# A two-layer transformer stack on one core: smaller work buffers, eight weight slots for eleven, 74 resident weight pieces for 68, a new order, and the local output projection in five chunks

## The chip, the cores and the metric

The kernel runs on one NeuronCore of a Trainium2 chip. The metric is the device time of one launch in microseconds; the time of a kernel is the median over several launches. Five engines work side by side and meet through semaphores: TensorE (PE, with its weight loads listed as PEld), VectorE (DVE), ScalarE (ACT), GpSimd (POOL) and SyncE (SP). SP here does nothing but issue weight transfers. Sixteen DMA engines carry all transfers between HBM and the on-chip memory SBUF; matrix products land in PSUM, which has eight banks.

## The reference

Two layers alternate, each used twice, on 2048 tokens of width 640, with a layer norm and a residual sum around each:

```python
x = x + _A_ref(_layernorm(x), A_mem0, A_Wq, A_Wk, A_Wv, A_Wo, A_seg_len)
x = x + _B_ref(_layernorm(x), B_wqkv, B_wo)
x = x + _A_ref(...)      # the same weights again
x = x + _B_ref(...)
```

Layer A is recurrent. The tokens come in 64 segments of 32. Eight memory rows are put in front of a segment, full attention with 32 heads of 192 runs over the 40 rows (causal behind the memory), and the eight first output rows are the memory of the next segment:

```python
for s in range(n_seg):
    h = concatenate([mem, xs[s]]);  q, k, v = h @ Wq, h @ Wk, h @ Wv
    p = softmax(where(mask, q @ k.T * scale, -1e9));  o = (p @ v) @ Wo
    mem = o[:, :M];  outs.append(o[:, M:])
```

Layer B is local attention: 32 heads of 20, each token sees eight tokens at distances 0, 2, ..., 14, then an output projection of 640 by 640.

## The kernel before

Both passes of A run at once, as two lanes of one matrix product: lane 0 has segment t of the first pass, lane 1 segment t - 2 of the second (LAG = 2). So a lane has 40 columns and a projection of A moves NT = 80 columns through each 128 by 128 weight block. In the first two steps and the last two of A only one lane is live. A step is one segment; there are 66 with A, and one more that has only B. B for the segment pair of step t - 1 runs inside step t.

A's heads are worked in eight quads of four heads. A step has these pieces, named in the string ORDER with the quad's number: K, Q, V (30 weight blocks each: project), KE, QE, VE (copy from PSUM to SBUF: KE and VE on ScalarE, QE on VectorE), T and TE (transpose V, copy), S (scores), E (exp, ScalarE), EM (mask, VectorE), PD (denominators), R (their reciprocals, as exp of minus Ln, both on ScalarE), PO (probabilities times V), OT1 and OT2 (divide, VectorE), Oa and Ob (output projection, 15 blocks each, into the two banks acc0 and acc1). Quad 7's output projection is split into O7x, O7y and O7z, so that acc0 is complete before acc1. MEMa and MEMb write the new memory rows from acc0 and acc1 into the next step's input hT; K0 of the next step reads it. X1 makes A's residual sum, BSQ its squares. LSQ, lst, LMV, LR and LAP are the layer norm of the next segment. Names in small letters are B's: bst to bap its layer norm, bq, bk, bv projections with bqE, bkE, bvE, then bt and btE, qx (queries spread over heads), bs (scores), be (exp, ScalarE), eb (mask, VectorE), bp and on (times V, divide), bo and boE (transpose), by (output projection) and byE (residual sum).

ORDER is a list written out in full. Each engine gets its instructions in that order and works them one after another; a piece waits only for semaphores of what it reads, and for the last readers of the buffers it writes. Five PSUM banks ("big") go round in the order in which pieces ask for them.

A's weights are 64 halves of 15 blocks, each half cut into pieces of 8 and 7 blocks (256 KB and 224 KB): 128 pieces. N_RES = 68 of them stay in SBUF after their first load in step 0. The other 60 are loaded again in each step, into a ring of RING = 11 slots (load_piece, the DMA is on line 220): SP issues the next transfer when TensorE is done with the slot's last content, and when the transfer eight before it has landed, because eight semaphores go round. `resident_pieces` picks the resident ones evenly by their number in the order of use. B's weights wqkv and wo are loaded once, after step 0.

Lines that matter below: 242 the projections of A, 361 its output projection, 391 the memory rows, 451 bq and bk, 552 bo, 566 by, 511 be and 522 eb, 332 R, 349 to 355 OT1 and OT2.

Of the kernel before, what the change touches and what calls it, by code (L numbers as in the profile page):

```python
# [17 lines left out]
P = 128  # L18
D = 640
# [26 lines left out]
PD0 PO0 R0 OT10 bq E1 Q4 bqE S2 EM1 V3 bv qx1 T2 QE4 E2 OT20 bk VE3 PO1 bvE qx0 PD1 T3 bkE K3 TE2 EM2 TE3 R1  # L46
KE3 bs0 be0 K4 OT11 OT21 bs1 be1 KE4 V5 Q3 QE3 eb1 PO2 VE5 bs3 PD2 V4 R2 qx2 S4 OT12 be3 VE4 E4 eb0 bs2 Oa1 S3
bt E3 EM4 K5 Q5 btE be2 bs5 eb3 Oa0 EM3 QE5 PD3 bs4 KE5 Q6 eb2 be5 eb5 OT22 Ob0 T4 S5 QE6 R3 PD4 be4 E5 PO3
eb4 OT13 K6 Ob1 TE4 bp1 T5 R4 V6 bp0 OT23 on1 PO4 KE6 TE5 EM5 VE6 S6 OT14 K7 Q7 E6 PD5 on0 OT24 T6 KE7 bo Oa2
# [16 lines left out]
def half_blocks(kind, i, h):  # L66
# [9 lines left out]
    return blocks[15 * h:15 * (h + 1)]  # L76

def resident_pieces():
    pieces = [u + (q,) for u in half_order() for q in range(2)]
    return {u for n, u in enumerate(pieces) if (n * N_RES) // len(pieces) != ((n + 1) * N_RES) // len(pieces)}  # L80

class Kernel:
# [25 lines left out]
    def build_consts(self):  # L108
# [24 lines left out]
        self.VT = pers("VT", [P, 6 * NT + 48], 2)  # L133
        self.x1 = pers("x1", [P, NC, NX], 2)
        self.h2T = pers("h2T", [P, NC, P], 1)[0]
        self.KB = pers("KB", [P, NBC, P], 1)[0]
# [6 lines left out]
        self.wqkv = cp.tile([P, NC, 3 * D], BF16, name="wqkv_sb")  # L143
        self.wo = cp.tile([P, 2, 3, D], BF16, name="wo_sb")

# [47 lines left out]
    def load_b_weights(self):  # L193
        nc = self.nc
        nc.sync.dma_start(out=self.wqkv[:].rearrange("p c n -> p (c n)"), in_=self.b_src[0])
        nc.sync.dma_start(out=self.wo[:].rearrange("p a m n -> p (a m n)"), in_=self.b_src[1])

# [112 lines left out]
    def sE(self, i):  # L310
        cs = self.cs
        e = self.ap1.tile([P, 4, NT], BF16, name="E", tag=f"E{i % 2}")
        self.nc.scalar.activation(out=e[0:NT, :, cs], in_=self.sv[i][0:NT, :, cs], func=ACT.Exp, scale=float(DH) ** -0.5)  # L313
        self.e[i] = e

    def sM(self, i):
        cs, w = self.cs, self.cs.stop - self.cs.start
        em = self.ap1.tile([P, 4, NT], BF16, name="Em", tag=f"Em{i % 2}")
        self.nc.vector.tensor_tensor(out=em[0:NT, :, cs], in0=self.e[i][0:NT, :, cs],  # L319
                                     in1=self.maskA[0:NT, cs].unsqueeze(1).to_broadcast([NT, 4, w]), op=ALU.mult)  # L320
        self.em[i] = em

# [109 lines left out]
    def b_x1(self, b):  # L432
        nc = self.nc
        x1 = self.x1[b % 2]
        ls = slice(self.l0, self.l1)
        for g, c in enumerate((slice(0, 3), slice(3, NC))):
            nc.vector.tensor_tensor(out=x1[:, c].rearrange("p c (l n) -> p c l n", l=2)[:, :, ls, :], in0=self.acc_lanes(g)[:, :, ls, NM:LT],
                                    in1=self.xin[b % 2][:, c].rearrange("p c (l n) -> p c l n", l=2)[:, :, ls, :], op=ALU.add)
        self.acc = None

    def b_ln_apply(self, b):
        self.ln_big(self.x1[b % 2], self.bmr, self.h2T[:, :, 64 * (b % 2):64 * (b % 2) + NX].rearrange("p c (l n) -> p c l n", l=2))

    def b_proj(self, b, col0, name):
        nc = self.nc
        ps = self.big(name)
        h = self.h2T[:, :, 64 * (b % 2):64 * (b % 2) + NX]
        for n in range(NBC):
            for c in range(NC):
                e0 = col0 + BHC * BD * n  # L450
                nc.tensor.matmul(ps[:, NX * n:NX * (n + 1)], lhsT=self.wqkv[:, c, e0:e0 + P], rhs=h[:, c, :],  # L451
                                 start=(c == 0), stop=(c == NC - 1))
        return ps
# [8 lines left out]

    def b_v(self, b):
        nc = self.nc
        ps = self.big("ps_bv")
        hs = slice(64 * (b % 2), 64 * (b % 2) + NX)
        for n in range(NC):
            for c in range(NC):
                e0 = 2 * D + P * n
                nc.tensor.matmul(ps[:, NX * n:NX * (n + 1)], lhsT=self.wqkv[:, c, e0:e0 + P], rhs=self.h2T[:, c, hs],  # L470
                                 start=(c == 0), stop=(c == NC - 1))
# [29 lines left out]
    def b_s(self, c):  # L501
# [4 lines left out]
        self.bsp[c] = ps  # L506

    def b_e(self, c):
        nh = min(BHC, BH - BHC * c)
        e = self.ap1.tile([P, BHC, NX], BF16, name="eraw", tag=f"eraw{c % 2}")  # L510
        self.nc.scalar.activation(out=e[:, 0:nh, :].rearrange("p h n -> p (h n)"), in_=self.bsp[c][:, 0:nh * NX], func=ACT.Exp, scale=float(BD) ** -0.5)  # L511
        self.be[c] = e

    def b_m(self, b, c):
        nc, e = self.nc, self.be[c]
        nh = min(BHC, BH - BHC * c)
        mask = self.maskB_first.get(b, self.maskB[b % 2])
        h = BHC * c
        end = h + nh
        while h < end:  # L520
            n = min(end, 16 if h < 16 else 32) - h
            nc.vector.tensor_tensor(out=self.eb[:, h % 16:h % 16 + n, h // 16, :], in0=e[:, h - BHC * c:h - BHC * c + n, :],  # L522
                                    in1=mask[:].unsqueeze(1).to_broadcast([P, n, NX]), op=ALU.mult)
            h += n

# [10 lines left out]
    def b_on(self, g):  # L536
        nc = self.nc
        pv = self.bpv[g]
        on = self.On[:, 0:D // 2].rearrange("p (h d) -> p h d", d=BD)
        r = self.ap2.tile([P, 8, 1], F32, name="rB")  # L540
        nc.vector.reciprocal(out=r[:], in_=pv[:, :, BD:BD + 1])
        for par in range(2):
            rows = slice(64 * par, 64 * par + 64)
            d0 = (BD + 1) * par
            nc.vector.tensor_tensor(out=on[rows, 8 * g:8 * g + 8, :], in0=pv[rows, :, d0:d0 + BD],  # L545
                                    in1=r[rows].to_broadcast([64, 8, BD]), op=ALU.mult)

    def b_ot(self):
        nc = self.nc
        ps = self.big("ps_bt")  # L550
        for m in range(3):
            nc.tensor.matmul(ps[:, P * m:P * (m + 1)], lhsT=self.On[:, P * m:P * (m + 1)], rhs=self.ident[:], start=True, stop=True)  # L552
        self.bop = ps

    def b_oE(self):
        ob = self.bp.tile([P, 3, P], BF16, name="OTB")
        self.nc.scalar.copy(out=ob[:], in_=self.bop[:, 0:3 * P].rearrange("p (m n) -> p m n", m=3))  # L557
        self.otb = ob

    def b_wo(self):  # L560
        nc = self.nc
        ps = self.big("ps_by")
        for n in range(NC):
            for k in range(6):
                par, m = k % 2, k // 2
                nc.tensor.matmul(ps[:, NX * n:NX * (n + 1)], lhsT=self.wo[:, par, m, P * n:P * (n + 1)],  # L566
                                 rhs=self.otb[:, m, 64 * par:64 * par + 64], start=(k == 0), stop=(k == 5))
        self.byp = ps

    def b_yE(self, b):  # L570
        nc = self.nc
        x1 = self.x1[b % 2]
        pv = self.byp[:, 0:NC * NX].rearrange("p (c n) -> p c n", c=NC)
# [21 lines left out]
    def prologue(self):  # L595
        nc = self.nc
        self.xt, self.ots, self.qxs, self.kp, self.qp, self.vp, self.tp = {}, {}, {}, {}, {}, {}, {}
        self.qt, self.e, self.em, self.r, self.bsp, self.be, self.bpv, self.sv, self.dn = {}, {}, {}, {}, {}, {}, {}, {}, {}
        self.acc = None
# [20 lines left out]
    def b_piece(self, n, b):  # L620
        k, g = n[:2], n[2:]
        if n == "bst":
            self.bsp_ = self.ln_stats(self.x1[b % 2], self.bsq)
        elif n == "bmv":
# [13 lines left out]
        elif n == "bv":  # L638
            self.b_v(b)
        elif n == "bvE":  # L640
# [27 lines left out]
    def a_piece(self, n, t):  # L668
# [8 lines left out]
        if n == "BSQ":  # L677
            self.bsq = self.ln_sq(self.x1[t % 2])
            return
# [63 lines left out]
def laid_out(A_x, A_mem0, A_Wq, A_Wk, A_Wv, A_Wo, B_wqkv, B_wo):  # L743
# [41 lines left out]
```

## Time and profile before

| | |
|---|---|
| median of 6 runs | 3391.9 us (3387.08 to 3402.63) |
| the profiled execution's own time | 3396.63 us |
| its span, first to last instruction | 3394.9 us |
| mean granted TensorE clock | 0.985 |
| HBM read, written | 1000.25 MB, 2.62 MB |
| step 0, step 1 | 83.7 us, 48.2 us |
| steps 5 to 63, together | 2971.0 us |

The page of the profile gives for each engine its busy time, share of the span and number of instructions, and for each DMA queue the packets, megabytes and share of the sixteen engines' span. A row of a group reads: line, engine, operation, output and inputs, shapes, count, then busy us and mean ns of one, then the idle time of the engine before it and what ended that. A row of the waits reads: who waited for whom, us in total, times, longest us. A row of the DMA issues ends in KB each and the median us from issue to landing. A row of the timeline begins with start and length in us.

### The profile page before, as it was taken

To read this page: it belongs to the slowest core of one execution; us is meant where nothing else is said; L and a number is where in the kernel's file an instruction comes from. 1 tells how busy PE (TensorE), PEld (TensorE's weight loads), DVE (VectorE), ACT (ScalarE), POOL (GpSimd) and SP (SyncE) were. 2 spreads that over 40 slices of the span, in tenths; PEclk is the share of its full clock that TensorE was granted. 3 is DMA by queue.
4 is the path that set the end of the run, shared out by engine and by line. 5 is a ranking of instruction groups with operands and counts; after the bars stand their busy time and mean duration, and the time that the engine had idled before them with its cause. 6 is when DMAs were issued, how large, how long until landed. Compare 5 with 4: busy or idle time off the path is not lost. (4 is left out here: it accounts for less than half of the span.)

```text
span 3394.9 us, 194049 instructions
## 1 busy us (share of the span) xinstructions
PE 3222.4 (95%) x86394; PEld 3145.7 (93%) x86394; DVE 2060.2 (61%) x6355; ACT 1742.1 (51%) x4621; POOL 40.7 (1%) x150
## 2 busy tenths in 40 slices
PE   5799999999999999999999999999999999999997
PEld 4799999999999999999999999999999999999986
DVE  2466665666666666566666666666656656656655
ACT  1355455455555555555545555555555555555543
POOL 2000000000000000000000000000000000000000
PEclk6899999999999999999999999999999999999998
DMA  9989999899999998898998999999899889889896
GB/s 326 334 299 300 301 295 300 302 297 310 297 303 300 305 308 292 299 306 291 301 306 293 305 300 305 301 299 306 292 296 299 295 295 305 294 294 303 285 308 217
DMA packets 585910, 1015.55 MB, mean 299 GB/s; under 512 B 65136, under 2 KB 310384, under 8 KB 584944
## 3 DMA queue, kind: packets, MB, share of 16 engines
q1 hardware_dynamic: 580320, 997.88, 88.3%
q8 instruction: 677, 11.09, 1.3%
q10 hardware_dynamic: 4752, 5.26, 0.4%
q14 instruction: 161, 1.32, 0.1%
HBM read 1000.25 MB, written 2.62 MB: 295 GB/s over the span
## 5 line engine op out<-in xcount | busy, mean ns | idle before, releaser
L242 PEld LDWEIGHTS <-w_ring 128*128 128x128 bf16 x22506 | 994.5, 100 | 61.0 <-issue 31.9
L277 DVE CAST QT<-ps_q 128x480 bf16<-128x480 f32 (+1 forms) x528 | 339.2, 642 | 470.9 <-PE ps_q L242 443.4
L349 DVE TENSOR_TENSOR OT<-ps_o,R 128x320 bf16<-128x320 f32 (+1 forms) x528 | 254.2, 481 | 303.4 <-ACT R L332 177.9
L282 ACT CAST VT_107<-ps_v 128x480 bf16<-128x480 f32 (+1 forms) x264 | 144.2, 546 | 413.6 <-PE ps_v L242 412.0
L313 ACT ACTIVATE E<-ps_s 80x320 bf16<-80x320 f32 (+1 forms) x528 | 223.2, 423 | 251.4 <-PE ps_s L307 251.2
L361 PEld LDWEIGHTS <-w_ring 128*128 128x128 bf16 x7326 | 331.1, 100 | 13.1 <-issue 4.9
L331 ACT ACTIVATE R<-ps_d 128x320 f32<-128x320 f32 (+1 forms) x528 | 226.5, 429 | 221.6 <-PE ps_d L325 218.9
L332 ACT ACTIVATE R<-R 128x320 f32<-128x320 f32 (+1 forms) x528 | 243.9, 462 | 16.7
L296 DVE COPY Vt_103<-ps_vt 80x384 bf16<-80x384 bf16 x528 | 163.3, 349 | 136.9 <-PE ps_vt L288 134.8
L242 PE MATMUL ps_q<-hT_88,w_ring 128*128 128x80 bf16 (+1 forms) x4026 | 231.3, 201 | 8.2 <-issue 6.0
L242 PE MATMUL ps_q<-hT_90,w_ring 128*128 128x80 bf16 (+1 forms) x4026 | 229.7, 201 | 5.4 <-issue 4.0
L242 PE MATMUL ps_v<-hT_88,w_ring 128*128 128x80 bf16 (+1 forms) x3795 | 218.6, 201 | 8.6 <-issue 4.2
L242 PE MATMUL ps_v<-hT_90,w_ring 128*128 128x80 bf16 (+1 forms) x3795 | 217.5, 201 | 7.0 <-issue 5.5
L282 ACT CAST VT_105<-ps_v 128x480 bf16<-128x480 f32 (+1 forms) x264 | 143.6, 544 | 155.5 <-PE ps_v L242 155.1
L242 PE MATMUL ps_k<-hT_90,w_ring 128*128 128x80 bf16 (+1 forms) x3432 | 197.6, 200 | 11.1 <-DMA w_ring<-in_wA_dram 8.6
L242 PE MATMUL ps_k<-hT_88,w_ring 128*128 128x80 bf16 (+1 forms) x3432 | 198.9, 201 | 5.3 <-DVE hT_88 L429 2.4
L271 ACT CAST KF_95<-ps_k 128x320 bf16<-128x320 f32 (+1 forms) x264 | 110.1, 417 | 179.3 <-PE ps_k L242 179.3
L271 ACT CAST KF_93<-ps_k 128x320 bf16<-128x320 f32 (+1 forms) x264 | 110.2, 418 | 165.9 <-PE ps_k L242 165.9
L319 DVE TENSOR_TENSOR Em<-E,maskA 80x320 bf16<-80x320 bf16 (+1 forms) x528 | 165.0, 313 | 43.5 <-ACT E L313 31.3
L296 DVE COPY Vt_101<-ps_vt 80x384 bf16<-80x384 bf16 x528 | 161.3, 345 | 43.4 <-PE ps_vt L288 43.4
L511 ACT ACTIVATE eraw<-ps_bs 128x384 bf16<-128x384 f32 (+1 forms) x396 | 175.3, 446 | 19.6 <-PE ps_bs L505 16.9
L355 DVE TENSOR_TENSOR OT<-ps_o,R 64x160 bf16<-64x160 f32 (+1 forms) x528 | 170.3, 322 | 7.2
(2830 smaller groups left out, 8699.9 us busy)
## 6 DMA issues: line engine op xcount, KB each, us to landing
w_ring<-in_wA_dram SPq DMA_DIRECT2D x2112, 256.0 KB, 4.7
w_ring<-in_wA_dram SPq DMA_DIRECT2D x1848, 224.0 KB, 4.8
out_dram<-YT_125 ACTq DMA_DIRECT2D x16, 160.0 KB, 5.4
wqkv_sb<-in_wqkv_dram SPq DMA_DIRECT2D x1, 2400.0 KB, 10.2
wo_sb<-in_wo_dram SPq DMA_DIRECT2D x1, 960.0 KB, 12.0
w_k_00_550<-in_wA_dram SPq DMA_DIRECT2D x1, 256.0 KB, 5.1
w_k_10_569<-in_wA_dram SPq DMA_DIRECT2D x1, 256.0 KB, 5.1
w_q_00_592<-in_wA_dram SPq DMA_DIRECT2D x1, 256.0 KB, 5.1
```

The costliest lines, as they stand in the source:

```text
L242: self.nc.tensor.matmul(ps[:, NT * n + c0:NT * n + c1], lhsT=self.block(kind, i, h, k), rhs=hT[:, NT * c + c0:NT * c + c1], start=(h == 0 ...
L271: nc.scalar.copy(out=kf[:, :, :, cs], in_=pv[:, :, 0:3:2, cs])
L277: self.nc.vector.tensor_copy(out=qt[:, :, self.cs], in_=self.qp[i][:, 0:6 * NT].rearrange("p (a n) -> p a n", a=6)[:, :, self.cs])
L282: self.nc.scalar.copy(out=vt[:, :, self.cs], in_=self.vp[i][:, 0:6 * NT].rearrange("p (a n) -> p a n", a=6)[:, :, self.cs])
L296: nc.vector.tensor_copy(out=dst[:, 512 * pr:512 * pr + 640].rearrange("p (j e) -> p j e", j=2)[:, :, 0:DH], in_=src[:, pr])
L313: self.nc.scalar.activation(out=e[0:NT, :, cs], in_=self.sv[i][0:NT, :, cs], func=ACT.Exp, scale=float(DH) ** -0.5)
L331: self.nc.scalar.activation(out=rf, in_=self.dn[i], func=ACT.Ln)
L332: self.nc.scalar.activation(out=rf, in_=rf, func=ACT.Exp, scale=-1.0)
L349: self.nc.vector.tensor_tensor(out=ot[:, :, 0:3:2, cs], in0=self.ov[:, :, 0:3:2, cs], in1=self.r[i][:, :, :, cs], op=ALU.mult)
L355: nc.vector.tensor_tensor(out=ot[64:P, :, 1, cs], in0=ov[64:P, :, 1, cs], in1=r[64:P, :, 1, cs], op=ALU.mult)
L361: self.nc.tensor.matmul(self.acc[c // 3][:, o:o + self.cs.stop - self.cs.start], lhsT=self.block("o", i, h, k), rhs=ot[:, m, self.cs], sta ...
L511: self.nc.scalar.activation(out=e[:, 0:nh, :].rearrange("p h n -> p (h n)"), in_=self.bsp[c][:, 0:nh * NX], func=ACT.Exp, scale=float(BD) ...
```

## The change

- `RING` goes from 11 to 8, `N_RES` from 68 to 74; 54 pieces are streamed in each step. `resident_pieces` now lays the pieces out along an estimate of TensorE's time (one unit a block, some units for each piece without weights) and streams the ones nearest to 54 evenly spaced points.
- ORDER has the same pieces in another order.
- E is written into the buffer of EM, and the mask is applied in place. R has one buffer instead of two. B's exp writes straight into EB, and its mask is applied there in place; chunk c = 2 of be, whose heads lie in both halves of EB, takes two instructions. x1 has one buffer instead of two, h2T 64 columns instead of 128.
- B's attention output is laid out so that its transpose gives five chunks of 128 rows; `b_ot` takes five matrix products instead of three, `b_wo` 25 instead of 30, and `wo` is stored in five chunks.

```diff
-RING = 11
-N_RES = 68
+RING = 8
+N_RES = 74
...
-K0 V1 K0y VE1 bst bmv KE0 Q0 QE0 V0 T1 K1 br TE1 VE0 bap Q1 QE1 S0 KE1 T0 E0 EM0 Q2 K2 V2 KE2 VE2 QE2 TE0 S1
...
-Ob2 boE R5 PO5 QE7 S7 V7 TE6 E7 VE7 EM6 OT15 by PD6 OT25 PO6 T7 R6 EM7 Oa3 byE Ob3 TE7 Oa4 PD7 LSQ lst OT16
-Ob4 OT26 LMV PO7 Oa6 R7 Oa5 OT17 LR Ob5 OT27 Ob6 LAP O7x MEMa O7y O7z MEMb X1 BSQ
+K0 Q0 K0y KE0 V0 QE0 K1 bst VE0 KE1 bmv S0 T0 V1 TE0 Q1 QE1 VE1 K2 E0 Q2 V2 br EM0 bap KE2 T1 PD0 QE2 S1 VE2
...
+boE PO5 T6 QE7 Ob2 EM6 R5 TE6 S7 OT15 PD6 OT25 E7 by V7 byE EM7 Ob3 PO6 PD7 R6 LSQ Oa4 VE7 T7 lst OT16 OT26
+TE7 R7 LMV Ob4 Oa6 LR PO7 Oa5 OT17 Ob6 OT27 Ob5 O7x O7y O7z LAP MEMa MEMb X1 BSQ
...
+NO_WEIGHTS = {"T": 4, "S": 3, "PD": 2, "PO": 3, "bst": 3, "lst": 3, "bq": 10, "bk": 10, "bv": 8, "bt": 3, "bo": 2, "by": 8, "bp": 2, "bs": 2}
 def resident_pieces():
-    pieces = [u + (q,) for u in half_order() for q in range(2)]
-    return {u for n, u in enumerate(pieces) if (n * N_RES) // len(pieces) != ((n + 1) * N_RES) // len(pieces)}
...
+    pieces = [(at[u] + 8 * q, u + (q,)) for u in half_order() for q in range(2)]
+    pieces.sort()
+    stream, n_s = set(), len(pieces) - N_RES
+    k = 0
+    for j in range(n_s):
+        want = (j + 0.5) * t / n_s
+        while k < len(pieces) - (n_s - j) and abs(pieces[k + 1][0] - want) <= abs(pieces[k][0] - want):
+            k += 1
+        stream.add(pieces[k][1])
+        k += 1
+    return {u for _, u in pieces} - stream
...
     def sE(self, i):
-        e = self.ap1.tile([P, 4, NT], BF16, name="E", tag=f"E{i % 2}")
+        e = self.ap1.tile([P, 4, NT], BF16, name="Em", tag=f"Em{i % 2}")
...
     def dR(self, i):
-        r = self.ap1.tile([P, 2, 2, NT], F32, name="R", tag=f"R{i % 2}")
+        r = self.ap1.tile([P, 2, 2, NT], F32, name="R")
...
+    def b_e(self, c):
+        for o, h, a, n in self.heads_of(c):
+            self.nc.scalar.activation(out=self.eb[:, h:h + n, a, :], in_=self.bsp[c][:, NX * o:NX * (o + n)].rearrange("p (h n) -> p h n", h=n),
+                                      func=ACT.Exp, scale=float(BD) ** -0.5)
...
     def b_ot(self):
-        for m in range(3):
-            nc.tensor.matmul(ps[:, P * m:P * (m + 1)], lhsT=self.On[:, P * m:P * (m + 1)], rhs=self.ident[:], start=True, stop=True)
+        on, ident = self.On, self.ident
+        for o, c, q in ((0, 0, 0), (64, 256, 1)):
+            nc.tensor.matmul(ps[:, o:o + 64], lhsT=on[:, c:c + P], rhs=ident[:, 64 * q:64 * q + 64], start=True, stop=True)
+        nc.tensor.matmul(ps[:, P:2 * P], lhsT=on[:, P:2 * P], rhs=ident[:], start=True, stop=True)
+        for c, q in ((256, 0), (0, 1)):
+            nc.tensor.matmul(ps[:, 256:320], lhsT=on[:, c:c + P], rhs=ident[:, 64 * q:64 * q + 64], start=(q == 0), stop=(q == 1))
...
     def b_wo(self):
         for n in range(NC):
-            for k in range(6):
...
+            for k in range(NC):
+                nc.tensor.matmul(ps[:, NX * n:NX * (n + 1)], lhsT=self.wo[:, k, P * n:P * (n + 1)],
+                                 rhs=self.otb[:, NX * k:NX * (k + 1)], start=(k == 0), stop=(k == NC - 1))
```

More of the change, by code (lines that the diff above doesn't have):

```diff
@@ L76, in half_blocks @@
     return blocks[15 * h:15 * (h + 1)]
+NO_WEIGHTS = {"T": 4, "S": 3, "PD": 2, "PO": 3, "bst": 3, "lst": 3, "bq": 10, "bk": 10, "bv": 8, "bt": 3, "bo": 2, "by": 8, "bp": 2, "bs": 2}
 def resident_pieces():
-    pieces = [u + (q,) for u in half_order() for q in range(2)]
-    return {u for n, u in enumerate(pieces) if (n * N_RES) // len(pieces) != ((n + 1) * N_RES) // len(pieces)}
+    at, t = {}, 0.0
+    for n in ORDER:
+        if n[0] in "KQV" and len(n) == 2 and n != "K0":
+            at.update({(n[0].lower(), int(n[1]), h): t + 15 * h for h in range(2)})
+        elif n == "K0":
+            at.update({("k", 0, h): t + 15 * h for h in range(2)})
+        elif n[:2] in ("Oa", "Ob"):
+            at[("o", int(n[2]), int(n[1] == "b"))] = t
+        elif n == "O7x":
+            at.update({("o", 7, h): t + 15 * h for h in range(2)})
+        t += 30 if len(n) == 2 and n[0] in "KQV" else 15 if n[0] == "O" and n[1] in "ab" else 30 if n == "O7x" else NO_WEIGHTS.get(n.rstrip("01234567"), 0)
+    pieces = [(at[u] + 8 * q, u + (q,)) for u in half_order() for q in range(2)]
[9 more added lines that the diff above has]
+    return {u for _, u in pieces} - stream
 class Kernel:
@@ L133, in build_consts @@
         self.VT = pers("VT", [P, 6 * NT + 48], 2)
-        self.x1 = pers("x1", [P, NC, NX], 2)
-        self.h2T = pers("h2T", [P, NC, P], 1)[0]
+        self.x1 = pers("x1", [P, NC, NX], 1)[0]
+        self.h2T = pers("h2T", [P, NC, NX], 1)[0]
         self.KB = pers("KB", [P, NBC, P], 1)[0]
@@ L143, in build_consts @@
         self.wqkv = cp.tile([P, NC, 3 * D], BF16, name="wqkv_sb")
-        self.wo = cp.tile([P, 2, 3, D], BF16, name="wo_sb")
+        self.wo = cp.tile([P, NC, D], BF16, name="wo_sb")
         mA = cp.tile([P, NT], BF16, name="maskA")
@@ L441, in b_ln_apply @@
     def b_ln_apply(self, b):
[L442 removed]
+        self.ln_big(self.x1, self.bmr, self.h2T[:].rearrange("p c (l n) -> p c l n", l=2))
     def b_proj(self, b, col0, name):
@@ L446, in b_proj @@
         ps = self.big(name)
-        h = self.h2T[:, :, 64 * (b % 2):64 * (b % 2) + NX]
+        h = self.h2T
         for n in range(NBC):
@@ L469, in b_v @@
                 e0 = 2 * D + P * n
-                nc.tensor.matmul(ps[:, NX * n:NX * (n + 1)], lhsT=self.wqkv[:, c, e0:e0 + P], rhs=self.h2T[:, c, hs],
+                nc.tensor.matmul(ps[:, NX * n:NX * (n + 1)], lhsT=self.wqkv[:, c, e0:e0 + P], rhs=self.h2T[:, c, :],
                                  start=(c == 0), stop=(c == NC - 1))
@@ L506, in b_s, with heads_of, b_m @@
         self.bsp[c] = ps
[L508 to L519, printed above, removed]
+    def heads_of(self, c):
+        h, end = BHC * c, min(BHC * (c + 1), BH)
         while h < end:
             n = min(end, 16 if h < 16 else 32) - h
-            nc.vector.tensor_tensor(out=self.eb[:, h % 16:h % 16 + n, h // 16, :], in0=e[:, h - BHC * c:h - BHC * c + n, :],
-                                    in1=mask[:].unsqueeze(1).to_broadcast([P, n, NX]), op=ALU.mult)
+            yield h - BHC * c, h % 16, h // 16, n
             h += n
+    def b_e(self, c):
+        for o, h, a, n in self.heads_of(c):
+            self.nc.scalar.activation(out=self.eb[:, h:h + n, a, :], in_=self.bsp[c][:, NX * o:NX * (o + n)].rearrange("p (h n) -> p h n", h=n),
+                                      func=ACT.Exp, scale=float(BD) ** -0.5)
+    def b_m(self, b, c):
+        mask = self.maskB_first.get(b, self.maskB[b % 2])
+        for o, h, a, n in self.heads_of(c):
+            e = self.eb[:, h:h + n, a, :]
+            self.nc.vector.tensor_tensor(out=e, in0=e, in1=mask[:].unsqueeze(1).to_broadcast([P, n, NX]), op=ALU.mult)
     def b_pv(self, g):
```

48 lines of the change are left out of this document (21 added, 27 removed).

## The prediction

> **What bounds the kernel now.** I read the page first (engines, clock, queues), then the busy times of the stretches between steps, what TensorE's weight loads waited for, and windows inside a step.
>
> ```profile
> span 3394.9 us, 194049 instructions
> PE 3222.4 (95%) x86394; PEld 3145.7 (93%) x86394; DVE 2060.2 (61%) x6355; ACT 1742.1 (51%) x4621; POOL 40.7 (1%) x150
> ...
> q1 hardware_dynamic: 580320, 997.88, 88.3%
> q8 instruction: 677, 11.09, 1.3%
> ...
> w_ring<-in_wA_dram SPq DMA_DIRECT2D x2112, 256.0 KB, 4.7
> w_ring<-in_wA_dram SPq DMA_DIRECT2D x1848, 224.0 KB, 4.8
> ```
>
> TensorE is busy nearly throughout, so a step can shrink only by what TensorE executes less, or stands idle less. A second reading matters more: q8 moves 11.09 MB for 2 x 86394 PE and PEld instructions, 64 bytes each. It is TensorE's program, coming in 677 packets of 16.4 KB, one per 86394/677 = 127.6 matmuls, beside the 997.88 MB of weights. Weights are 2112 + 1848 = 3960 transfers, 60 a step over 66 steps, 14.8 MB a step.
>
> The stretches (us, then busy us and instructions of PE, PEld, DVE, ACT, POOL, then clock, DMA share, GB/s) are step 0, step 1, steps 5 to 63, step 64 and step 65:
>
> ```profile
> 22.70:106.40 83.70, 56.81 (x1154) 46.77 (x1153) 18.51 (x69) 15.47 (x58) 0.41 (x1) 0.57 1.00 361
> 106.40:154.60 48.20, 40.97 (x1309) 39.33 (x1310) 24.67 (x92) 19.84 (x70) 0.00 (x0) 0.90 0.95 327
> ...
> 307.10:3278.10 2971.00, 2889.89 (x77234) 2832.55 (x77232) 1857.41 (x5664) 1580.33 (x4130) 21.32 (x58) 1.00 0.91 300
> 3278.10:3325.50 47.40, 38.73 (x1313) 37.39 (x1310) 26.07 (x96) 19.93 (x70) 0.00 (x0) 0.96 0.92 312
> 3325.50:3373.50 48.00, 37.70 (x1299) 36.37 (x1299) 23.64 (x88) 19.34 (x68) 0.00 (x0) 1.00 0.84 281
> ```
>
> A steady step takes 2971.00/59 = 50.36 us; PE idles 81.1 us in the 59, 1.37 us a step, at full clock. What PEld waited for in the same stretch:
>
> ```profile
> PEld L242 <- issue: 50.0, 76, 2.0
> PEld L451 <- issue: 16.4, 19, 1.9
> ...
> PEld L242 <- DMA w_ring<-in_wA_dram: 2.6, 3, 1.5
> ...
> PEld L505 <- issue: 0.3, 1, 0.3
> L242 PEld LDWEIGHTS <-w_ring 128*128 128x128 bf16 x22506 | 994.5, 100 | 61.0 <-issue 31.9 <-DMA w_ring<-in_wA_dram 20.4
> ```
>
> The eleven "issue" rows (two and the last shown) make 95.0 us in 145 idles; waits for weights make 2.6 us. "Issue" means that nothing in the profile held the engine. Each idle also hides the 64 ns by which the recorded 100 ns of a weight load (last row, all steps) exceed the 36 ns from one 80-column matmul to the next (98 of them in 3.55 us in the step tail below), so I count 95.0 + 145 x 0.064 = 104 us, 1.8 us a step (PE idle bounds it at 1.37, PEld's whole idle time, 138.5/59, at 2.35).
>
> What are they? The windows below run each from the end of one such idle to the end of a later one:
>
> ```profile
> 1122.39:1126.92 4.54, 4.37 (x127) 4.24 (x127) 3.18 (x9) 2.81 (x8) 0.00 (x0) 1.00 0.97 329
> 1126.92:1147.01 20.09, 19.74 (x511) 19.11 (x511) 12.66 (x40) 13.19 (x35) 0.00 (x0) 1.00 0.93 298
> 1147.01:1175.42 28.41, 28.05 (x765) 27.78 (x766) 18.05 (x55) 12.82 (x35) 0.38 (x1) 1.00 0.94 318
> ```
>
> 127, 511 and 765 matmuls are 1, 4 and 6 times 127.6: the idles fall on the packet boundaries of q8. **TensorE waits for its own instructions, and those come through DMA engines that the weights keep busy.** When do they come late? Four windows at 5 to 15 us of a step, then four at its last 10 us:
>
> ```profile
> 666.10:676.10 10.00, 8.81 (x245) 8.63 (x243) 5.06 (x14) 4.62 (x13) 0.00 (x0) 1.00 1.03 369
> 1265.11:1275.11 10.00, 9.29 (x259) 9.15 (x256) 5.14 (x15) 4.78 (x14) 0.00 (x0) 1.00 1.02 354
> 1869.49:1879.49 10.00, 9.57 (x262) 9.34 (x260) 5.26 (x15) 4.92 (x14) 0.00 (x0) 1.00 1.00 359
> 2470.93:2480.93 10.00, 9.12 (x254) 8.98 (x252) 5.09 (x14) 4.73 (x13) 0.00 (x0) 1.00 1.00 355
> 700.95:710.95 10.00, 10.00 (x281) 9.92 (x278) 7.32 (x24) 4.40 (x11) 0.00 (x0) 1.00 0.87 274
> 1300.46:1310.46 10.00, 10.00 (x282) 9.92 (x279) 7.31 (x24) 4.40 (x11) 0.00 (x0) 1.00 0.84 261
> 1904.38:1914.38 10.00, 10.00 (x281) 9.92 (x279) 7.33 (x24) 4.41 (x11) 0.00 (x0) 1.00 0.85 267
> 2506.49:2516.49 10.00, 9.72 (x270) 9.50 (x266) 6.89 (x23) 3.94 (x10) 0.00 (x0) 1.00 0.86 271
> ```
>
> Early in a step projections follow one another, the DMA engines are full (355 to 369 GB/s, share 1.00 and over), and PE idles 3.2 of 40 us. At the end, at 261 to 274 GB/s, it idles 0.28 of 40 us.
>
> **The change, part by part.** *Streaming.* 54 pieces a step in place of 60 are 13.3 MB; over a step of 49 us that is 272 GB/s, and they are chosen at even distances in TensorE's time, where before every other piece in order was streamed, however dense the pieces stood. So the whole step should look like its last 10 us do now: 0.28/40 x 49 = 0.34 us of PE idle against 1.37, a quarter. Of 1.8 us a step I let 0.45 stay: **-1.35 us**. Bounds: all goes (-1.8, or -2.35 by PEld), or it falls only with the bytes (-0.17, rival A).
>
> *Eight slots in place of eleven.* A slot comes round after 8 x 49/54 = 7.26 us, less 0.29 for the eight matmuls that read it: 6.97 us in which SP must see the release, issue and land the next piece. Landing takes 4.7 to 4.8 us now, issuing 0.33 us:
>
> ```profile
> L220 SPq DMA_DIRECT2D w_ring<-in_wA_dram x3960: 327/328/2305, 0.8 to 3365.6; - x198
> ...
> SPq L220 <- DMA w_ring<-in_wA_dram: 171.0, 495, 3.1
> ```
>
> [...] I cost it at nothing; without the room it is the slower rival. SP now waits 495 times, 171 us in steps 5 to 63, because its eighth-last transfer has not landed; these waits should shrink.
>
> *Output projection and transpose.* From the timeline of one step:
>
> ```profile
> 1554.08 1.04 PE L566 MATMUL ps_by<-OTB,wo_sb 128*128 128x64 bf16 x30
> ...
> 1550.80 0.33 PE L552 MATMUL ps_bt<-ident,On_122 128*128 128x128 bf16 x3
> L566 PE MATMUL ps_by<-OTB,wo_sb x1980: 189/193/242, 147.2 to 3391.6; 128*128 128x64 bf16 x198
> L552 PE MATMUL ps_bt<-ident,On_122 x198: 217/219/314, 145.2 to 3389.2; 128*128 128x128 bf16 x198
> ```
>
> A 64-column matmul follows its predecessor after (1.04 - 0.193)/29 = 29 ns, a 128-column one after (0.33 - 0.219)/2 = 55 ns. b_wo loses five of the first kind (-146 ns); b_ot goes from three of the second to four of the first and one of the second (+6 ns): **-0.14 us**.
>
> *Order.* One place has no room left. The tail of a step today:
>
> ```profile
> 1558.30 0.46 PE L342 MATMUL ps_o<-Em,Vt_103 80*128 80x80 bf16 x8
> ...
> 1560.54 0.56 DVE L429 TENSOR_TENSOR hT_88<-ln_xc,ln_r 128x160 bf16<-128x160 f32 x2
> ...
> 1561.59 0.21 DVE L391 CAST hT_88<-ps_acc_51433 128x48 bf16<-128x48 f32 x1 [0.49 <-PE ps_acc_51433 L361]
> 1561.85 0.45 PE L242 MATMUL ps_k<-hT_88,w_ring 128*128 128x80 bf16 x8
> ```
>
> From PO7 (1558.30) VectorE works OT17, OT27 and LAP until 1561.10, 2.80 us later, then MEMa (0.21) frees K0. Today 98 matmuls stand between PO7's start and K0, 3.55 us, and MEMa waits for O7x. In the new order Oa6 stands ahead of PO7, so 83 remain, 83 x 36 = 2.97 us, while VectorE's chain needs 2.80 + 0.21 + 0.06 = 3.07: K0 waits **+0.10 us** (bounds 0 and 0.3). Elsewhere the new order keeps producers well ahead of consumers.
>
> *The buffers.* E joins Em, so a score exp waits for PO of two quads earlier, not for the mask; one R lets Ln wait for the OT2 before it; B's exp writes EB and waits for bp1 of the previous step; x1 and h2T have one buffer, overwritten after their last reader in program order. ScalarE gains one exp a step (c = 2 in two parts, at most one more 0.28 us start):
>
> ```profile
> L511 ACT ACTIVATE eraw<-ps_bs 128x128 bf16<-128x128 f32 x66 | 18.3, 277 | 15.2 <-PE ps_bs L505 14.7 <-DVE EB_124 L522 0.5
> ```
>
> ScalarE (51%) and VectorE (61%) have that time free under TensorE; all this costs nothing unless ScalarE's queue is held at an R, when S, K and V evictions behind it come late and TensorE misses a PSUM bank (up to 0.3 us a step).
>
> *Start and end.* Step 0 loads all 128 pieces at 361 GB/s, share 1.00, either way: 0. Steps 1, 64 and 65 have one lane, hence 40-column matmuls, yet take 47 to 48 us with PE idle 7 to 10 us. There TensorE outruns its fetches, and a faster step raises the load again; I take a third of the idle, 3 us each: -9 us (bounds 0 and -27).
>
> Sum: steps 2 to 63 go from 50.36 to 50.36 - 1.35 - 0.14 + 0.10 = 48.97 us; 62 x 1.39 = 86; with 9, **95 us**. The profiled execution took 3396.6 (span 3394.9); 3301.6 is forecast for it. The median, 3391.9, lies 4.7 lower: **3297 us**.
>
> **The rivals.** *A: the fetch waits for one weight packet, however many stand behind.* Then idle falls only with the rate, 272/300: 1.8 x 0.09 = 0.17 us, with -0.04 from the matmuls 0.21 x 62 + 3 = 16 us: **3376**. For it: share falls only from 0.91 to about 0.83. Against: between the windows above share falls by a sixth, idle by a factor of eleven. [...]
>
> *B: the idles are not the fetch's delay.* Then only 62 x 0.04 = 2.5 us goes: **3389**. [...]
>
> *C: eight slots are too few (slower).* If release to landing takes 7.3 us where 6.97 are there, each turn loses 0.33 us, 54/8 turns a step 2.2 us; less 1.39 gained, +0.84 x 62 = 52: **3444**. It decides from 6.97 + 1.39 x 8/54 = 7.2 us on. For it: SP's 495 waits say that eight transfers are often outstanding. [...]
>
> **How the numbers follow.** Forecast 0.79, A 0.10, B 0.05, C 0.06. The range runs from all 2.35 us of idle gone (62 x 2.39 = 148, less 10 for the waits of the new order: **3254**) to half of the idle staying with no gain at the ends (62 x 0.94 = 58, less an R stall of 0.3 us in every step, 19, gives 3353; taken a little into A): **3364**. A change below 0.2% (6.8 us) can't be told from none. Faster is the forecast and A, 0.89; the same B, 0.05; slower C, 0.06.
>
> **What would show it.** q1 with 54 x 66 = 3564 transfers and some 900 MB; "issue" idles of PEld in the steady steps down from 95 us to about a quarter; landings under 4.7 us; GB/s near 272 in windows early and late in a step alike; L566 with 1650 matmuls; K0 waiting 0.1 us for L391. The prediction is wrong if PEld waits for w_ring by more than some 20 us (C), if "issue" stays above 80 us at DMA shares near 0.83 (A), or if TensorE waits for ScalarE or VectorE in the middle of a step.

## The result, and the profile after

The changed kernel takes 3294.7 us (median of 10; 3288.0 to 3298.7) against 3393.5 us before (20 runs): a ratio of 0.9707, 95% interval 0.9694 to 0.9720. Forecast were 3297 us. The profiled execution took 3287.7 us, 14 us less than the 3301.6 forecast for it.

The page after, its first lines, weight queue and transfers:

```profile
span 3286.0 us, 192807 instructions
PE 3193.5 (97%) x86196; PEld 3127.8 (95%) x86196; DVE 2028.5 (62%) x6354; ACT 1727.6 (53%) x4687; POOL 41.0 (1%) x150
...
q1 hardware_dynamic: 524160, 903.97, 85.6%
q8 instruction: 675, 11.06, 1.4%
...
w_ring<-in_wA_dram SPq DMA_DIRECT2D x1980, 256.0 KB, 4.2
w_ring<-in_wA_dram SPq DMA_DIRECT2D x1584, 224.0 KB, 4.1
```

3564 transfers, 904 MB, and a landing takes 4.2 us where it took 4.7. TensorE's program comes in 675 packets, where it came in 677. Line numbers have moved with the change: 242 is 264 here, 342 is 363, 361 is 382, 391 is 412, 429 is 450, 451 is 472. The stretches of the span, columns as in the prediction (step 0, step 1, steps 5 to 63, step 64, step 65):

```profile
22.80:97.20 74.40, 56.63 (x1155) 46.14 (x1155) 17.86 (x65) 15.20 (x58) 0.00 (x0) 0.60 1.01 363
97.20:150.70 53.50, 38.71 (x1311) 37.32 (x1309) 25.11 (x98) 19.70 (x71) 0.41 (x1) 0.89 0.93 320
296.88:3175.80 2878.92, 2866.50 (x77056) 2819.49 (x77054) 1828.66 (x5664) 1567.68 (x4189) 21.41 (x58) 1.00 0.88 280
3175.80:3221.30 45.50, 38.18 (x1308) 36.54 (x1306) 25.67 (x98) 19.80 (x71) 0.00 (x0) 1.00 0.90 293
3221.30:3268.40 47.10, 39.36 (x1296) 38.02 (x1296) 23.32 (x89) 19.09 (x69) 0.00 (x0) 0.93 0.83 268
```

| stretch | before, us | after, us | difference |
|---|---|---|---|
| steps 0 and 1 | 131.9 | 127.9 | -4.0 |
| steps 2 to 4 | 152.5 | 146.2 | -6.3 |
| steps 5 to 63 | 2971.0 | 2878.9 | -92.1 |
| steps 64 and 65 | 95.4 | 92.6 | -2.8 |
| step 66 (B alone) | 21.4 | 17.6 | -3.8 |

A steady step went from 50.36 to 2878.92/59 = 48.80 us, PE's idle time from 1.37 to 12.4/59 = 0.21 us a step. What the weight loads waited for in steps 5 to 63, all rows:

```profile
PEld L264 <- issue: 10.7, 22, 1.3
PEld L363 <- issue: 2.0, 4, 0.8
PEld L382 <- issue: 1.4, 2, 0.8
PEld L310 <- issue: 0.9, 3, 0.6
PEld L472 <- issue: 0.9, 2, 0.5
PEld L264 <- DMA w_ring<-in_wA_dram: 0.4, 1, 0.4
PEld L328 <- issue: 0.3, 1, 0.3
```

"Issue" fell from 95.0 us in 145 idles to 16.2 us in 34; weights are hardly waited for, with three slots fewer. Three windows at 5 to 15 us of a step, then two at its last 10 us, of the same steps as the first ones of each kind in the prediction:

```profile
644.47:654.47 10.00, 10.00 (x279) 9.92 (x276) 6.32 (x21) 6.06 (x17) 0.00 (x0) 1.00 0.88 291
1230.31:1240.31 10.00, 10.00 (x273) 9.86 (x270) 6.16 (x20) 5.92 (x17) 0.00 (x0) 1.00 0.92 283
1816.42:1826.42 10.00, 10.00 (x279) 9.92 (x276) 6.32 (x21) 6.05 (x17) 0.00 (x0) 1.00 0.96 310
677.92:687.92 10.00, 10.00 (x276) 9.87 (x273) 7.63 (x26) 4.62 (x11) 0.00 (x0) 1.00 0.89 279
1264.26:1274.26 10.00, 10.00 (x276) 9.87 (x273) 7.62 (x26) 4.61 (x11) 0.00 (x0) 1.00 0.83 257
```

The early part of a step, which ran at 354 to 369 GB/s in such windows, is down to 283 to 310, the DMA share to 0.88 to 0.96 from 1.00 and over, and PE has no idle time there.

### The profile page after: what moved, and what is told of

Read it like the earlier page. It is cut to its first block, busy times and chain, and to the rows that moved or that the text cites. A ratio compares the mean times of both kernels' runs of the same rounds, so it can differ in the third digit from the quotient of the medians.

```text
span 3286.0 us, 192807 instructions
## 1 busy us (share of the span) xinstructions
PE 3193.5 (97%) x86196; PEld 3127.8 (95%) x86196; DVE 2028.5 (62%) x6354; ACT 1727.6 (53%) x4687; POOL 41.0 (1%) x150
## 4 chain that ended last, share of the span: by engine, by line
PE 95%; DMA 2%; issue 1%; DVE 0%; POOL 0%; ACT 0%; SPq 0%; POOLq 0%; DVEq 0%
PE ps_k L264 17%; PE ps_q L264 17%; PE ps_v L264 17%; PE ps_vt L310 5%; PE ps_o L363 5%; PE ps_s L328 2%; PE ps_s L329 2%; PE ps_d L346 2%; PE ps_bq L472 2%; PE ps_bk L472 2%; PE ps_bs L525 2%; PE ps_by L589 2%; DMA w_ring<-in_wA_dram 1%; PE ps_bv L490 1%; PE ps_st L424 1%
## 5 line engine op out<-in xcount | busy, mean ns | idle before, releaser
L264 PEld LDWEIGHTS <-w_ring 128*128 128x128 bf16 x20922 | 932.1, 100 | 53.0 <-DMA w_ring<-in_wA_dram 19.2
L382 PEld LDWEIGHTS <-w_ring 128*128 128x128 bf16 x6006 | 267.3, 100 | 7.9 <-issue 3.4
L335 ACT ACTIVATE Em<-ps_s 80x320 bf16<-80x320 f32 (+1 forms) x528 | 225.2, 426 | 76.2 <-PE ps_s L329 70.8
L341 DVE TENSOR_TENSOR Em<-Em,maskA 80x320 bf16<-80x320 bf16 (+1 forms) x528 | 164.6, 312 | 139.1 <-ACT Em L335 135.9
L264 PE MATMUL ps_q<-hT_88,w_ring 128*128 128x80 bf16 (+1 forms) x3564 | 202.9, 201 | 3.8 <-DMA w_ring<-in_wA_dram 3.0
L264 PE MATMUL ps_q<-hT_90,w_ring 128*128 128x80 bf16 (+1 forms) x3564 | 203.0, 200 | 2.8 <-issue 2.8
L264 PE MATMUL ps_v<-hT_88,w_ring 128*128 128x80 bf16 (+1 forms) x3432 | 193.4, 201 | 5.0 <-issue 2.8
L264 PE MATMUL ps_v<-hT_90,w_ring 128*128 128x80 bf16 (+1 forms) x3432 | 192.3, 200 | 1.2 <-issue 1.2
L537 ACT ACTIVATE EB_122<-ps_bs 128x384 bf16<-128x384 f32 (+2 forms) x462 | 171.7, 414 | 8.6 <-PE ps_bs L525 1.6
```

What stands on the lines that cost most here:

```text
L264: self.nc.tensor.matmul(ps[:, NT * n + c0:NT * n + c1], lhsT=self.block(kind, i, h, k), rhs=hT[:, NT * c + c0:NT * c + c1], start=(h == 0 ...
L382: self.nc.tensor.matmul(self.acc[c // 3][:, o:o + self.cs.stop - self.cs.start], lhsT=self.block("o", i, h, k), rhs=ot[:, m, self.cs], sta ...
L537: self.nc.scalar.activation(out=self.eb[:, h:h + n, a, :], in_=self.bsp[c][:, NX * o:NX * (o + n)].rearrange("p (h n) -> p h n", h=n), fun ...
```

## The experiments

Each kernel was timed beside the kernel before on one chip, so the ratio is what counts. The traces are of single executions, on chips where the kernel before took 3393 to 3408 us. Two traces of the changed kernel, "after" and "after, once more" below, differ by 0.11 us in the steady step (48.80 and 48.91), so smaller differences between traces say nothing. Those on the streaming in one table; the columns after the ratio are PEld's idle time in steps 5 to 63 while it waited for nothing that the profile shows ("issue", sums of all its rows) and while it waited for weights.

| kernel | MB a step, slots, choice | ratio to before | issue, us | weights, us |
|---|---|---|---|---|
| before | 14.8, 11, by number | 1 | 95.0 | 2.6 |
| after | 13.4, 8, even | 0.9707 (0.9694 to 0.9720) | 16.2 | 0.4 |
| after, once more | 13.4, 8, even | 0.9712 (0.9685 to 0.9740) | 21.9 | 0.9 |
| half the bytes | 7.9, 11, by number | 0.9576 (0.9557 to 0.9595) | 0.0 | 0.0 |
| 12.8 MB | 12.8, 11, by number | 0.9717 (0.9678 to 0.9756) | 22.2 | 0.4 |
| 13.8 MB | 13.8, 11, by number | 0.9864 (0.9845 to 0.9884) | 53.8 | 2.0 |
| even choice alone | 14.5, 10, even | 0.9903 (0.9876 to 0.9930) | 79.7 | 0.0 |
| eight slots alone | 14.8, 8, by number | 1.0147 (1.0128 to 1.0166) | 47.1 | 72.5 |
| after, by number | 13.3, 8, by number | 0.9835 (0.9811 to 0.9859) | 31.7 | 18.7 |
| after, 68 resident | 14.7, 8, even | 0.9920 (0.9898 to 0.9942) | 46.0 | 26.2 |
| after, six slots | 13.4, 6, even | 0.9981 (0.9968 to 0.9994) | 2.8 | 90.7 |

**Half the bytes.** Does the weight traffic make the idles at all? Only the length of the transfers changes, and which block of a piece a matmul reads:

```diff
-        self.nc.sync.dma_start(out=t_[:, 0:w], in_=src)
+        n = w if res or self.t == 0 else 4 * P
+        self.nc.sync.dma_start(out=t_[:, 0:n], in_=src[:, 0:n])
...
+            if self.t:
+                k %= 4
```

> The kernel before, but from step 1 on only the first four blocks of each streamed piece are loaded and they are used twice (so the output is another one): the same instructions on every engine and the same 60 transfers a step, with 7.9 MB a step in place of 14.8. Theory F (TensorE's instruction packets are late because weight transfers stand ahead of them): the issue idles all but go, a steady step falls from 50.4 to 48.4-48.7 us, steps 1, 64 and 65 lose most of their idle too, total 3250-3275 us. Rival A (idle goes with the bytes): 0.53 of 1.8 us stay, total about 3330. Rival B (the idles are not the DMA engines' doing): 3385-3395.

3257.5 us. Steps 5 to 63 (busy columns as above):

```profile
294.11:3154.62 2860.51, 2860.51 (x77235) 2822.18 (x77232) 1857.13 (x5664) 1578.68 (x4130) 21.30 (x58) 1.00 0.58 168
```

PE is busy for all 2860.51 us; the list of PEld's waits in this stretch is empty. 2860.51/59 = 48.48 us is what a step of the old instructions takes when nothing is late. So the prediction's 1.8 us of loss a step was 50.36 - 48.48 = 1.88. Theory F holds. Rival A's straight line (3330 us) and rival B (3385 to 3395 us) are out.

The traces also list every DMA packet with its queue, start and length, and those of q8 show what TensorE waited for. In the kernel before, the number of matmuls ahead of each of the 145 issue idles is 127.61 n + 222, where n is the number of the q8 packet that ended last; the error is less than one matmul in all 145. Each of these idles ends 1.0 to 1.6 us after that packet. The packet's own transfer is no slower under load: its median is 0.96 us before and after, and 1.03 us with half the bytes. What is late is its start. It comes a median 1.98 us after TensorE has begun the 128 matmuls ahead of the packet's own (2.90 us for the 145 late packets), 1.36 us in the changed kernel (1.51 in its second trace), 0.41 us with half the bytes. None of the 605 packets in the steady steps of the kernel before starts ahead of those 128 matmuls; the earliest comes 0.04 us behind their begin. What holds the start up on its way, these lists don't say.

**How steeply.** The same edit with seven of eight and six of seven blocks, as shown, then with (7, 7) in both places:

```diff
-        self.nc.sync.dma_start(out=t_[:, 0:w], in_=src)
+        n = w if res or self.t == 0 else P * (7, 6)[q]
+        self.nc.sync.dma_start(out=t_[:, 0:n], in_=src[:, 0:n])
...
+            if self.t:
+                k %= (7, 6)[q]
```

> The kernel before, 60 streamed pieces chosen by number through 11 slots, but from step 1 on seven of eight and six of seven blocks of each are loaded and the first block is used twice (another output): 12.8 MB a step in place of 14.8 (the changed kernel: 13.4), in the same places. If the idle falls steeply with the amount, whatever the density: 3280-3310 us. If density counts as much: 3315-3340. If idle falls straight with the bytes between 14.8 MB (3392) and 7.9 MB (3257): 3350-3365.

> The kernel before, but from step 1 on seven blocks of every streamed piece are loaded, of the larger ones with the first used twice (another output): 13.8 MB a step, chosen by number, 11 slots. With 14.8 MB the steady step takes 50.4 us, with 12.8 MB 49.0. If the idle grows steadily between them: 49.7 us a step, 3340-3360 us. If it sets in steeply near 14.8 MB: 49.2 us a step or less, 3305-3330.

3309.3 and 3348.6 us. Steps 5 to 63 of the first and of the second:

```profile
301.52:3192.15 2890.63, 2873.62 (x77235) 2827.10 (x77233) 1856.83 (x5664) 1581.12 (x4130) 21.40 (x58) 1.00 0.85 268
```

```profile
301.19:3227.94 2926.75, 2879.81 (x77235) 2829.46 (x77232) 1856.37 (x5664) 1581.39 (x4130) 21.31 (x58) 1.00 0.88 283
```

A step takes 48.99 us at 12.8 MB and 49.61 at 13.8, so beyond the 48.48 of an undisturbed one 0.51, 1.13 and, at 14.8, 1.88 us. From 12.8 to 14.8 MB each further MB costs 0.6 to 0.8 us a step; at 7.9 MB nothing is left. In the second kernel the loss grows steadily, as the milder of its two expectations had it; the first lies at the upper end of "steeply with the amount". There the old uneven places, the old order and eleven slots leave 22.2 us of issue idles, as many as the changed kernel has in its second trace (21.9). So at 12.8 MB the amount alone is enough. But the changed kernel moves 13.4 MB. There the line between the two rows gives a loss of some 0.9 us a step (an estimate), and the changed kernel has 0.4 to 0.5: 48.80 or 48.91 us less an undisturbed step of 48.43 (48.48, less 0.14 for the output projection, plus 0.09 for K0's wait, both measured below). By this estimate the amount makes some 70% of the gain, and the places, the slots and the new order together the rest. No run changes the order alone, so its share stays open.

**The even choice alone.** The changed `resident_pieces` in the kernel before, and one slot less:

```diff
-RING = 11
+RING = 10
...
-    pieces = [u + (q,) for u in half_order() for q in range(2)]
-    return {u for n, u in enumerate(pieces) if (n * N_RES) // len(pieces) != ((n + 1) * N_RES) // len(pieces)}
+    pieces = [(at[u] + 8 * q, u + (q,)) for u in half_order() for q in range(2)]
+    pieces.sort()
...
```

> The kernel before with the changed choice of streamed pieces (evenly in TensorE's time), still 68 resident pieces; 10 slots, since the choice leaves a little more resident and SBUF is full. 14.5 MB a step in place of 14.8. If the density of the streamed pieces makes the fetches late (theory F as forecast): more than half of the gain, 3310-3345 us. If the amount alone does (A): 3380-3390.

3371.2 us, ratio 0.9903: neither more than half of the gain nor none of it. In its trace the steady step is 2951.80/59 = 50.03 us:

```profile
304.43:3256.23 2951.80, 2889.93 (x77235) 2831.05 (x77232) 1857.84 (x5664) 1581.31 (x4130) 21.43 (x58) 1.00 0.91 296
```

0.33 us less than before; by the ratio, 1.0% or 33 us, it would be some 0.5 us a step. By the loss per MB above, 0.3 MB less accounts for some 0.2 us of it (an estimate). So the even places, with one slot less, give 0.1 to 0.3 us a step by themselves at this amount, of a loss of 1.88.

**The even choice undone in the changed kernel.**

```diff
-    pieces = [(at[u] + 8 * q, u + (q,)) for u in half_order() for q in range(2)]
-    pieces.sort()
...
+    pieces = [u + (q,) for u in half_order() for q in range(2)]
+    return {u for n, u in enumerate(pieces) if (n * N_RES) // len(pieces) != ((n + 1) * N_RES) // len(pieces)}
```

> The changed kernel with the old choice of streamed pieces (evenly by their number), 74 resident, 8 slots, 13.3 MB a step. If density counts (F): dense stretches come back, 3315-3345 us against 3295. If the amount alone counts (A): 3290-3300.

3346.6 us, ratio 0.9835: 1.3% are lost again, though 13.3 MB are moved; the time lies at the upper end of what F expected. The first two rows of PEld's waits in steps 5 to 63:

```profile
PEld L242 <- issue: 18.7, 29, 1.3
PEld L242 <- DMA w_ring<-in_wA_dram: 18.7, 39, 1.5
```

Beside later fetches there is a wait that neither kernel had to this extent (2.6 and 0.4 us): for the weights themselves. Here eight slots were enough for 54 pieces at even distances (0.4 us of waits), and not for the same number chosen by number (18.7 us).

**68 resident pieces in the changed kernel.**

```diff
-N_RES = 74
+N_RES = 68
```

> The changed kernel with 68 resident pieces in place of 74: 60 streamed ones of 14.7 MB a step, spread evenly, through 8 slots. F with density: 3310-3345 us; amount alone: 3380 or more. A slot comes round in 8 x 49.5/60 = 6.6 us less 0.3, and release to landing takes some 5 us: waits of the weight loads for w_ring stay under 15 us in the steady steps; rival C (slots too few at this rate): over 60 us of such waits and a time above 3392.

3375.6 us, ratio 0.9920. The waits for w_ring, 26.2 us in all, lie between the two expectations, and the time too.

```profile
PEld L264 <- issue: 29.5, 54, 1.5
PEld L264 <- DMA w_ring<-in_wA_dram: 23.9, 57, 1.6
```

**Eight slots alone, in the kernel before.**

```diff
-RING = 11
+RING = 8
```

> The kernel before with 8 slots in place of 11 and nothing else. Where every other piece is streamed and projections follow one another, a slot comes round in some 8 x 0.54 = 4.3 us, less than release to landing takes (about 5 us): the weight loads wait for w_ring by 0.5 us a step or more, in part where they waited for instructions. If what is lost there is gained in earlier fetches: 3380-3400 us. If slots are simply too few (C): 3410-3450. If the depth doesn't matter: waits for w_ring stay below 5 us in all.

3444.1 us: 1.5% slower, ratio 1.0147 (1.0128 to 1.0166). This is rival C, in the kernel before, and its time (3444) to the microsecond, which is chance.

```profile
PEld L242 <- DMA w_ring<-in_wA_dram: 70.5, 119, 1.5
PEld L242 <- issue: 22.6, 45, 1.6
```

72.5 us of waits for weights came; of the 95.0 us of issue idles about half (47.1) stayed. Part of what was lost to weights came back in instruction fetches, not all.

**Six slots in the changed kernel.**

```diff
-RING = 8
+RING = 6
```

> The changed kernel with 6 slots: a slot comes round in 6 x 48.8/54 less 0.3 = 5.1 us; landing takes 3.8 us on the mean, with issue and release about 4.3, and one in ten takes 0.9 us longer. C: waits for w_ring of 1 to 2 us a step, 3350-3430 us. Rival (fewer outstanding transfers pay it back): 3290-3305.

3389.7 us, ratio 0.9981: nearly the whole gain is gone, inside the range for C.

```profile
PEld L264 <- DMA w_ring<-in_wA_dram: 85.8, 143, 2.0
PEld L382 <- DMA w_ring<-in_wA_dram: 4.9, 13, 0.9
PEld L382 <- issue: 1.5, 4, 0.6
PEld L264 <- issue: 0.8, 3, 0.5
```

Issue idles are down to 2.8 us at an unchanged 13.4 MB a step: the instruction packets are on time (they start a median 1.17 us after the 128 matmuls ahead of their own, against 1.36), but then the weights are not. Whether that comes of fewer transfers outstanding, or of a TensorE that waits for weights and so gives its fetches time, no run separates.

**Five chunks alone.** The changed `b_on`, `b_ot`, `b_oE`, `b_wo` and layout of `wo` in the kernel before.

```diff
-            for k in range(6):
+            for k in range(NC):
...
```

> The kernel before with only the output projection and the transpose in five chunks. By the count of matmuls 0.14 us a step, 9 us, 3382 against 3392 (ratio 0.997). Rival: the time a step loses to late instruction packets grows by what the projection saves, because the transfers of a step take as long as before: ratio 0.999 to 1.000.

3391.6 us (12 runs), ratio 0.9954, interval 0.9934 to 0.9973. The count of matmuls (0.997) lies at the upper edge, the rival of no gain outside. The trace shows the term itself. From the first matmul of by to the first of the next piece it takes 0.731 us in place of 0.877 (medians of 59 steps), and of bo 0.172 in place of 0.167: together -0.14 us, as counted. The whole step is only 0.06 us shorter in that trace (2967.97/59 = 50.30 us, with 99.1 us of issue idles), a difference too small for two traces from different chips: the kernel before took 3407.5 us (median of 17 runs) on the chip of this one, and 3393.5 on that of the changed kernel.

**The tail.** LAP's subtraction moved ahead of OT17 on VectorE:

```diff
-TE7 R7 LMV Ob4 Oa6 LR PO7 Oa5 OT17 Ob6 OT27 Ob5 O7x O7y O7z LAP MEMa MEMb X1 BSQ
+TE7 R7 LMV Ob4 Oa6 LR LX PO7 Oa5 OT17 Ob6 OT27 Ob5 O7x O7y O7z LAP MEMa MEMb X1 BSQ
...
+        elif n == "LX":
+            self.axc = self.ln_sub(x, self.amr[0])
```

> The changed kernel with LAP's subtraction taken out of the chain behind OT27 and put ahead of OT17 on VectorE. If the wait of K0 for the memory rows is the 0.12 us a step that its start shows, it goes: 62 x 0.12 = 7 us, 0.2% below the changed kernel, a steady step 48.7 us in place of 48.8. If something else holds K0 by then: no difference, and K0 still waits for L412.

> The changed kernel once more, beside the one with the shorter tail, on one chip: ratio to the kernel before 0.969 to 0.973.

3298.8 us against 3306.6 us for the changed kernel on the same chip, ratios 0.9686 (0.9657 to 0.9715) and 0.9712 (0.9685 to 0.9740). The 7.8 us are about the 7 us that were expected, but the intervals overlap, so the times alone don't settle it. The timeline does for the wait. First the tail of step 29 in the changed kernel, then the same place with the subtraction moved:

```profile
1514.64 0.46 PE L363 MATMUL ps_o<-Em,Vt_103 80*128 80x80 bf16 x8
...
1516.89 0.56 DVE L450 TENSOR_TENSOR hT_88<-ln_xc,ln_r 128x160 bf16<-128x160 f32 x2
...
1517.48 0.21 DVE L412 CAST hT_88<-ps_acc_50640 128x48 bf16<-128x48 f32 x1
1517.74 0.45 PE L264 MATMUL ps_k<-hT_88,w_k_00_379 128*128 128x80 bf16 x8
```

```profile
1521.77 0.21 DVE L412 CAST hT<-ps_acc 128x48 bf16<-128x48 f32 x1 [0.54 <-PE ps_acc L382]
...
1522.03 0.45 PE L264 MATMUL ps_k<-hT,w_k 128*128 128x80 bf16 x8
```

In the changed kernel MEMa starts when VectorE is done with LAP; with the subtraction moved VectorE has been idle for 0.54 us and waits for TensorE, as before the change. It is so in every steady step: K0's first matmul starts 0.15 to 0.16 us after the matmul ahead of it in the changed kernel, and 0.07 us with the subtraction moved, as in the kernel before. So the wait was 0.09 us a step, and it is gone. The steady step is 0.07 us shorter than in the trace of the changed kernel on the same chip (48.84 and 48.91 us), which is no more than two traces of one kernel differ by.

**One slot for one more resident piece**, on top of that:

```diff
-RING = 8
-N_RES = 74
+RING = 7
+N_RES = 75
```

> The changed kernel with the shorter tail, one slot traded for one more resident piece: 7 slots, 53 streamed pieces a step, 12.9 MB. Fetch waits fall by some 0.1 us a step; a slot comes round in 7 x 48.7/53 less 0.3 = 6.1 us on the mean. Six slots (5.1 us) cost 1.8 us a step in waits for w_ring, eight (6.9 us) nothing: halfway some 0.3 to 0.8 us, 3310-3340 us beside 3299 for the one with eight slots. Rival: 7 slots are still enough, 3288-3298.

3293.4 us, ratio 0.9682 (0.9648 to 0.9717): the same as with eight slots (0.9686), as the rival had it. The waits for w_ring were overestimated: 11.1 us, 0.19 a step, and the issue idles fell to 9.4 us, so the sum, 20.5 us, is that of eight slots with the shorter tail (19.4 and 1.1). From eight slots and 54 pieces to seven and 53, the one wait grows by what the other loses. Neither version is faster than the changed kernel beyond the intervals.

## Why the prediction was right, and where it was not

*What bounds the kernel.* Right, and now shown: TensorE stood idle for its own instruction packets, and weight traffic made them late. Leaving out half of the bytes removed every such idle with the same instructions (95.0 us in steps 5 to 63 at 300 GB/s, none at 168 GB/s), and each of the 145 idles of the kernel before ends 1.0 to 1.6 us behind the q8 packet whose matmuls come next.

*Streaming, -1.35 us.* The size was about right. With the matmuls saved (0.14) and K0's wait (0.09), the step fell by 1.56 us, or by 1.45 in the second trace, against 1.39 forecast, so this term came to -1.4 to -1.5. The reason given for it was only half right. The step that failed is "the whole step should look like its last 10 us do now" because the pieces are chosen at even distances. The rate is not flat at 272 GB/s (283 to 310 early, 279 and 257 late), and the idle is gone all the same. Even choice alone gave 1.0% at 14.5 MB, the amount alone 2.8% at 12.8 MB. What failed with it is rival A's arithmetic, the only form in which the amount alone stood there: loss doesn't fall in proportion to the bytes but at 0.6 to 0.8 us a step for each MB between 12.8 and 14.8, of a total of 1.88.

Two steps of the working were loose. The 272 GB/s are the weights alone, while the 300 and the windows count all queues; so counted the steady steps run at 280 now. And the 10 us taken off at the lower end of the range for waits of the new order follow from nothing shown, since the 2.39 holds those 0.10 us a step already; nothing else rests on it.

*Eight slots, costed at nothing.* Right for this kernel (0.4 us of waits): the landing became shorter (4.2 us, from 4.7) and SP's waits for a landing went from 171 us in steps 5 to 63 to 17 us in the whole span.

```profile
SPq L242 <- DMA w_ring<-in_wA_dram: 17.2, 56, 1.1
```

The cost of nothing stood on an estimate of how long a piece takes from release to landing, in which the time for SP to see a release is shown by no run. What the traces show is the whole way: from the end of the releasing matmul to the landing it takes a median of 4.4 us in the kernel before (one in ten over 5.5; the 2195 transfers of steps 5 to 63 whose issue begins within 0.06 us of that end) and 4.2 us in the changed kernel (2792 such). The issue's 0.33 us are in these, as they are in the 4.7, since the page counts a landing from the start of its issue. Yet the cover was thinner than the 6.97 us of a turn beside them says, since that is a mean over a step. Without the even choice weights are waited for by 18.7 us, with 60 pieces by 26.2, with both and the order as before by 72.5. The even choice belongs to this term more than to the one before: it lets eight slots do. How much it also helps the fetches can't be read off cleanly, because issue idles are fewer where weights are waited for (47.1 us in place of 95.0 with eight slots in the kernel before, 2.8 in place of 16.2 with six in the changed one). The half-loaded pieces of the dose kernels are shorter as well, so the 16.2 us after and the some 40 us that lie between their rows at 13.4 MB (an estimate, interpolated from 53.8 and 22.2) are no clean comparison either.

*Output projection, -0.14 us.* Right: the two pieces take 0.14 us less in the traces. Timed alone the change gives 0.5%, interval 0.3 to 0.7%, and the 0.27% that 9 us make lies at its lower end; whether it gives more than its matmuls stays open.

*K0's wait, +0.10 us.* Right: from PO7's start to the end of LAP the changed kernel takes 1517.45 - 1514.64 = 2.81 us (2.80 forecast), and K0 waits 0.09 us a step, which the moved subtraction removes.

*Buffers.* Right: no wait of PEld for ScalarE or VectorE stands in the steady steps of the changed kernel's trace.

*Start and end.* -9 us forecast for steps 1, 64 and 65. Steps 64 and 65 gave 2.8. Step 1 became longer by 5.3 and step 0 shorter by 9.3; only their sum, -4.0, can be compared, as the border between them moved. Step 66, which the sum leaves out, gave 3.8 us, but single traces differ by as much there: it takes 19.1 us in the second trace of the changed kernel, and 19.1 to 21.5 us in the runs with the old order and the old output projection. The granted clock in it was 0.62 before, 0.83 after and 0.75 after, once more.

*The rivals.* A and B fell with the half-loaded pieces. C is real for the kernel before, where eight slots cost 1.5%, and begins again in the changed one between seven slots (0.19 us a step) and six (90.7/59 = 1.54 us).

## What to carry to other kernels

Idle time of TensorE that the profile put down to "issue", at distances of 127.6 matmuls and multiples of it, was its program arriving late in this kernel; count instructions between two such idles and compare with the instruction queue's packets (677 for 86394 matmuls here). It went away with fewer bytes in flight beside it (95.0 us at 14.8 MB a step, none at 7.9), so a streamed byte cost time although instructions hardly waited for it (2.6 us). The shallower ring was paid for by even distances between its users: with eight slots the changed kernel waited 0.4 us for weights, and 18.7 us with pieces chosen by number. So judge a ring by the densest stretch and by release to landing, and not by the mean over a step.

## What the runs showed that was not expected

The response is steep: 13% of the bytes of a step (14.8 to 12.8 MB) carry 73% of the loss ((1.88 - 0.51)/1.88), with DMA shares of 0.91 and 0.85, both far from idle. What the load delays is not the instruction packet's transfer (0.96 us before and after) but its start (a median 1.98 us after TensorE began the 128 matmuls ahead of its own, 1.36 us in the changed kernel, 0.41 us with half the bytes). And the two kinds of wait trade against one another through the number of slots alone: at 13.4 MB a step, eight slots have 16.2 us of issue idles and 0.4 us of weight waits, six slots 2.8 and 90.7.
